# An output projection with twelve of its sixteen row tiles in Strassen's form, on one Trainium2 core

## The chip, the cores and the metric

The kernel runs on one core of a Trainium2 chip. The engines are named as in the profile: PE (TensorE, the matrix engine; PEld are its weight loads), DVE (VectorE), ACT (ScalarE), POOL (GpSimd) and SP (SyncE, which here only issues DMAs). The metric is the time of one execution on the device in microseconds, the median of several runs. Row times such as 1690.58 are microseconds from the start of the profiled span.

## The reference

The input x has 2048 rows (tokens) of 640 columns. The result mixes two blocks with a gate:

```python
g = sigmoid((x * gate_w).sum(-1, keepdims=True))
# a: attention, 32 heads of 20 columns
q, k, v = split(x @ wqkv)
p = softmax(q @ k.T * 20 ** -0.5)          # for each head
a = concat_heads(p @ v) @ wo               # the output projection, 640 x 640
# b: an MLP across the tokens
h = layernorm(x)                           # over the columns
b = (gelu(h.T @ w1 + b1) @ w2 + b2).T      # w1: 2048 x 1728, w2: 1728 x 2048
return g * a + (1 - g) * b
```

The change concerns `@ wo` alone: o, the heads' results (2048 x 640), times wo.

## The kernel before

**Precision.** Every float32 operand of a product is split into a high and a low part (`hi_lo`), and a product of two operands is three products on PE: high x high, high x low, low x high. One "product" below is one such matrix instruction.

**Stages.** First come the projections to q, k and v, then the MLP, together with part of the score maxima, then the attention loop: 16 pairs of heads (p), 32 iterations (it) each, in which ACT takes the exponentials. The attention's unnormalised results go to DRAM (`o_d`), the row sums to `l_d`, and the reciprocals of the row sums, repeated for each of a head's 20 columns, to `r_d`; for the last four heads (`LAST`) the reciprocals go to `rc_d` in a single copy, and are spread when they are read. The value projection in an early stage already has Strassen's form (`v_sums`, `v_head`, `v_body`, `v_tail`; `v_mm` at L498 writes its products): two row tiles by two halves of the contraction by two halves of the columns, seven sub-products instead of eight, with sums of x made on POOL and sums of the weights made on DVE.

**The output projection.** o is read back from DRAM transposed, as blocks of 128 columns of o (the contraction, five blocks) by rows. A *pair* q is 256 rows, two row tiles of 128. `e_load(q)` reads the first four blocks of pair q and the matching reciprocals (two loads of 512 KB, in two buffers each); `e_high` multiplies them and makes the high part, `e_low` the low part. The fifth block has its own tiles, of 512 rows each: `l_load` reads it with the reciprocals that are in `r_d`, `l_rest` reads the last four heads' reciprocals from `rc_d`, broadcast over the 20 columns of each head, `l_high` and `l_low` normalise and split. wo is loaded and split during the loop (`load_wo`, L1073) into `woh` and `wol`.

In the loop's last pair of heads `first_row` computes tile 0 and half of tile 1 (four blocks) between the attention's products, and POOL normalises pairs 0 to 2 (`e_high`, `e_low` at it 5, 20, 25). After the loop the other half of tile 1 is computed, then `pv_flush` finishes the attention, and then tiles 2 to 15 follow in order. `a_tile` (L1263) issues a tile's products: 24 for four blocks (four blocks x three passes x two halves of 320 columns), six more for the fifth block, which is accumulated with the rest from tile 8 on and done apart for tiles 0 to 7. Each tile takes its two PSUM banks in turn from four sets (`two`; `one1` and `one0`; the two `s`; `s3` and `pv`), and the `evac` that it returns multiplies by the gate and adds to the MLP's share (`tys`, loaded by `y_load`) on DVE, one instruction for each 320 columns (L1290). The row tile is stored when it is complete.

**What sets the order.** From L368 on ACT and DVE, from L455 on POOL and SP, and from the beginning PE run in the order in which the code issues (`manual_schedule`). Each of these five queues works in order; what the queues wait for follows from the tiles. The last reciprocals come late: the row sums of the last pair are stored after `pv_evac`, read back (`last_load`, L1019), inverted on DVE (`last_recip`, L1025), stored to `rc_d` from ACT's queue and read from there four times by `l_rest`.

## Time and profile before

| | |
|---|---|
| median of the runs | 1761.11 us (3 runs, 1760.94 to 1762.33) |
| the profiled execution | 1759.53 us |
| its span, first to last instruction | 1757.7 us |
| granted TensorE clock | 1.00 |
| PE busy | 1750.8 us |
| ACT busy | 1489.7 us |
| DVE busy | 1251.8 us |
| weight loads (PEld) | 1082.7 us |
| POOL busy | 682.6 us |
| DMA | 229.39 MB, mean 131 GB/s |

The page's busy time of an engine is the time in which at least one of its instructions ran. Matrix instructions overlap each other, so a row's duration is longer than the step from one to the next. A row of a timeline has start, length, engine, line of the kernel, instruction, result <- operands, shapes and count; in brackets stands the idle time of that engine just before it, and what released it. The DVE rows of L1290 are the evacuations. Queue rows (SPq, ACTq, POOL DMA) are issues of transfers, not the transfers.

### The profile page before, as it was taken

What the parts mean: (1) busy time and instruction counts of PE and PEld (TensorE: products, weight loads), DVE (VectorE), ACT (ScalarE), POOL (GpSimd) and SP (SyncE); (2) the same over time, 40 slices, a digit from 0 to 9 for tenths busy, and PEclk for the clock granted to TensorE, in tenths of its full rate; (3) what the DMA queues carried; (4) which work ended last, traced back from release to release, by engine and by line L of the source; (5) the groups of instructions that cost most, each with busy time, mean ns of one, the idle gap of its engine ahead of it and who ended that gap; (6) DMA issues with size and microseconds to landing.
All of it is one profiled execution on the core that took longest, in us unless ns stands there. A gap on an engine that the chain in (4) does not pass through costs nothing.

```text
span 1757.7 us, 39430 instructions
## 1 busy us (share of the span) xinstructions
PE 1750.8 (100%) x14972; PEld 1082.7 (62%) x14972; DVE 1251.8 (71%) x2443; ACT 1489.7 (85%) x2547; POOL 682.6 (39%) x936
## 2 busy tenths in 40 slices
PE   9999999999999999999999999999999999999999
PEld 7898899999999999533333333333333333333379
DVE  6633399988999899677767776776777777767336
ACT  5444388888888886899999999999999999999941
POOL 1434587789887777111211111121322122111410
PEclk9999999999999999999999999999999999999999
DMA  9868865476675564424313224043263144301445
GB/s 328 298 231 265 281 174 157 141 191 195 188 195 150 142 195 132 106 62 107 66 38 91 48 66 98 13 104 79 46 144 71 31 101 75 72 20 44 143 145 183
DMA packets 160945, 229.39 MB, mean 131 GB/s; under 512 B 66684, under 2 KB 97292, under 8 KB 157328
## 3 DMA queue, kind: packets, MB, share of 16 engines
q1 hardware_dynamic: 142606, 199.10, 40.6%
q0 software_dynamic: 14928, 21.86, 5.2%
q10 hardware_dynamic: 3220, 5.90, 1.1%
q8 instruction: 118, 1.93, 0.5%
q14 instruction: 73, 0.60, 0.1%
HBM read 171.07 MB, written 55.36 MB: 129 GB/s over the span
## 4 chain that ended last, share of the span: by engine, by line
PE 99%; DVE 0%; DMA 0%; ACT 0%; issue 0%; SPq 0%; ACTq 0%; DVEq 0%
PE pv L1065 29%; PE st L1164 23%; PE s L213 11%; PE y L49 10%; PE u L49 10%; PE qk L55 8%; PE v L501 4%; PE a L1284 1%; PE a_one L1284 1%; PE a_pv L1284 1%; PE a_s L1284 1%; PE a L49 0%; DMA xr<-in_xT_dram 0%; DVE mx L219 0%; PE y L894 0%
## 5 line engine op out<-in xcount | busy, mean ns | idle before, releaser
L219 DVE TENSOR_REDUCE mx<-s 128x1 f32<-128x512 f32 x1280 | 835.2, 687 | 281.8 <-PE s L213 147.0
L1182 ACT ACTIVATE p<-st 128x512 f32<-128x512 f32 x1022 | 560.5, 612 | 0.0
L1065 PE MATMUL pv<-p,v 128*32 128x512 f32 x4088 | 544.5, 605 | 0.0
L1171 ACT ACTIVATE p<-st 128x1024 f32<-128x1024 f32 x511 | 529.8, 1037 | 1.2 <-PE st L1164 1.1
L1164 PEld LDWEIGHTS st<-qs_True,ks_True 62*128 62x128 f32 x2044 | 243.8, 185 | 432.9 <-ACT p L1171 426.8
L1164 PE MATMUL st<-qs_True,ks_True 62*128 62x512 f32 x2044 | 494.0, 445 | 0.0
L213 PE MATMUL s<-ks_False,qs_False 60*128 60x512 f32 x1152 | 318.5, 391 | 0.3 <-ACT p L1182 0.2
L44 POOL TENSOR_TENSOR wl<-wr,wh 128x512 fp32r<-128x512 f32 x228 | 275.3, 1218 | 61.9 <-ACT wh L41 48.8
L238 DVE CUSTOM_DVE_ANT_0 ov<-s,ov 128x512 f32<-128x512 f32 x384 | 264.0, 688 | 36.5 <-PE s L213 25.2
L228 ACT ACTIVATE ov<-s 128x512 f32<-128x512 f32 x384 | 228.8, 598 | 62.4 <-PE s L213 54.3
L213 PE MATMUL s<-sk,sq 60*128 60x512 f32 x896 | 281.4, 394 | 0.0
L1046 POOL DMA_DIRECT2D l_d<-oev x124 | 60.4, 494 | 390.5 <-DVE oev L1038 387.8
L49 PE MATMUL y<-gh,wh 64*128 64x320 f32 x896 | 198.1, 305 | 0.0
L1065 PEld LDWEIGHTS pv<-p,v 128*32 128x32 f32 x4088 | 80.5, 108 | 187.0 <-issue 175.3
L49 PE MATMUL y<-gh,wl 64*128 64x320 f32 x832 | 191.6, 305 | 0.0
L49 PE MATMUL y<-gl,wh 64*128 64x320 f32 x832 | 191.5, 305 | 0.0
L213 PEld LDWEIGHTS s<-ks_False,qs_False 60*128 60x128 f32 x1152 | 189.0, 184 | 2.9 <-ACT p L1182 0.7
L49 PE MATMUL u<-hh,wh 64*128 64x320 f32 x864 | 186.0, 304 | 0.0
L49 PE MATMUL u<-hl,wh 64*128 64x320 f32 x864 | 185.9, 304 | 0.0
L41 ACT ACTIVATE wh<-wr 128x512 fp32r<-128x512 f32 (+3 forms) x247 | 146.8, 598 | 41.6 <-DMA wr<-in_wqk_dram 15.5
L213 PEld LDWEIGHTS s<-sk,sq 60*128 60x128 f32 x896 | 166.2, 186 | 14.9
L49 PE MATMUL u<-hh,wl 64*128 64x320 f32 x800 | 174.6, 305 | 0.0
(217 smaller groups left out, 2424.2 us busy)
## 6 DMA issues: line engine op xcount, KB each, us to landing
wr<-in_w_dram SPq DMA_DIRECT2D x192, 256.0 KB
ks_True<-k_d SPq DMA_DIRECT2D x96, 160.0 KB
qs_True<-q_d SPq DMA_DIRECT2D x192, 80.0 KB
qs_False<-q_d SPq DMA_DIRECT2D x96, 80.0 KB
v_d<-vt SPq DMA_DIRECT2D x32, 212.0 KB
sk<-k_d SPq DMA_DIRECT2D x42, 160.0 KB
sq<-q_d SPq DMA_DIRECT2D x84, 80.0 KB
v<-v_d SPq DMA_DIRECT2D x15, 424.0 KB
```

What stands on the lines that cost most here:

```text
L41: nc.scalar.activation(hi, src, AF.Copy)
L44: (lo_eng or nc.vector).tensor_sub(lo, src, hi.bitcast(F32))
L49: nc.tensor.matmul(ps[k], a[r], b[r], start=start, stop=stop)
L55: nc.tensor.matmul(ps, a, b, start=(i == 0 and k == 0), stop=(i == n - 1 and k == 2))
L213: nc.tensor.matmul(ps, qs[half][r, t * P:(t + 1) * P], ks[r, kc * 512:(kc + 1) * 512], start=True, stop=True)
L219: nc.vector.tensor_reduce(mx[:, slot, j, t: t + 1], ps, axis=AX.X, op=OP.max)
L228: nc.scalar.activation(over[j, kc], ps, AF.Relu)
L238: nc.vector.tensor_tensor_reduce(ov, ps, ov, 1.0, -3.0e38, OP.add, OP.max, mx[:, slot, j, t: t + 1])
L1065: nc.tensor.matmul(pv[r: r + 32, :], v_tiles[p][:, kt, VW * j: VW * j + 32], pt[j, c], start=(kt == 0), stop=(kt == NT - 1))
L1164: nc.tensor.matmul(ps, ks[r, kt * P:(kt + 1) * P], qs[qh][r, c * 512:(c + 1) * 512], start=True, stop=True)
L1171: nc.scalar.activation(pt, ps, AF.Exp, scale=SCALE)
L1182: nc.scalar.activation(pt, ps, AF.Exp, scale=SCALE)
```

## The change

Tiles 4 to 15, that is pairs 2 to 7, get Strassen's form over the first four blocks. For a pair, X, Y and Z are three PSUM banks of 320 columns. X takes the first product, then, accumulating, T2, T3 and T4, and is read by an evacuation after each of the four; Y takes one product, Z the product of T1 and later the one with the fourth sum of the weights. The sums of o (T1 to T4) are made by `t_sums` on POOL and split by `t_split` (high part on ACT, low part on DVE). `pair` issues a pair's first five sub-products and, in between, the last two (`foot`) of the pair before it. The sums of wo are made on POOL in the loop (`wo_load` at pair 14, it 8; `wo_sum` at pair 14, it 16, 20, 24, and pair 15, it 11).

Pair 3 is normalised on POOL in the loop, as pairs 0 to 2 are, and its load moves from it 29 to it 23; `t_sums` for pairs 2 and 3 follow there. Pairs 4 to 7 are normalised by `prep`: multiplication, sums and low part on POOL, high part on ACT, where DVE had the multiplication and the low part before. The fifth block is accumulated with the rest for tiles 8 to 15 in three of four half-tiles; the fourth (odd tile, right half) and tiles 0 to 7 (`fifth`) have products of their own, in the two banks of the tile `two`. Tile 3 is computed in two halves inside pair 2. `l_rest(3)` and `l_rest(1)` are issued after `prep(4)`, and the tiles of `l_high` come from other pools.

The core of the diff:

```diff
+    def t_sums(q):
+        raw, rb = o_keep[q]
+        r11, r12, r21, r22 = (raw[:, 2 * k: 2 * k + 2, n * P:(n + 1) * P] for k in range(2) for n in range(2))
+        t = [rb[:, j].rearrange("p (k s) -> p k s", k=2) for j in range(4)]
+        nc.gpsimd.tensor_sub(t[T1], r12, r11)
+        nc.gpsimd.tensor_sub(t[T2], r22, t[T1])
+        nc.gpsimd.tensor_sub(t[T3], r22, r12)
+        nc.gpsimd.tensor_sub(t[T4], r21, t[T2])
+    def t_split(q):
+        raw, rb = o_keep.pop(q)
+        hi, lo = t_hl[q] = t_tiles[q % 2]
+        hi_lo(hi, lo, rb, hi_eng=nc.scalar)
...
+    def wo_sum(n):
...
+        nc.gpsimd.tensor_tensor(dst, a, b, op=op)
...
+        hi_lo(hi, lo, dst, hi_eng=nc.gpsimd, lo_eng=nc.gpsimd)
...
+            if p == NP - 2 and it == 8:
+                wo_load()
+            if p == NP - 2 and it in (16, 20, 24):
+                wo_sum((it - 16) // 4)
             if p == NP - 1:
-                if it in (0, 14, 18, 29):
-                    e_load((0, 14, 18, 29).index(it))
+                if it == 11:
+                    wo_sum(3)
+                if it in (0, 14, 18, 23):
+                    e_load((0, 14, 18, 23).index(it))
...
+                if it in (5, 20, 25, 27):
+                    q = (5, 20, 25, 27).index(it)
+                    e_high(q, lp if q >= 2 else ap, nc.gpsimd)
+                    if q >= 2:
+                        o_keep[q] = o_raw[q, "e"]
                     e_low(q, nc.gpsimd)
+                    if q >= 2:
+                        t_sums(q)
...
+    def prep(q):
...
+        nc.gpsimd.tensor_mul(raw, raw, rb)
+        nc.scalar.activation(oh, raw, AF.Copy)
+        t_sums(q)
+        nc.gpsimd.tensor_sub(ol, raw, oh.bitcast(F32))
...
+    def ev(t, i, ps):
+        cols = slice(i * HALF, (i + 1) * HALF)
+        nc.vector.scalar_tensor_tensor(tys[t][:, cols], ps, g_t[:, t:t + 1], tys[t][:, cols], op0=OP.mult, op1=OP.add)
+        got(t, i)
...
+    def pair(q, fill=(), filler=()):
+        t0, t1 = 2 * q, 2 * q + 1
+        five = q >= Q0
+        X, Y, Z = o_ps[q] = [o_bank(q, k) for k in range(3)]
+        v_mm(X, [(o_x(q, 0, k), o_w(0, k)) for k in range(2)], True)
+        ev(t0, 0, X)
+        v_mm(Y, [(o_x(q, 0, 2 + k), o_w(0, 2 + k)) for k in range(2)] + [(l_x(t0), o_w(0, NC - 1)) for _ in range(five)], True)
+        ev(t0, 0, Y)
+        if q > X0:
+            foot(q - 1, 0)
+        for f in fill[:1]:
+            f()
+        v_mm(X, [(o_t(q, T2, k), o_s(2, k)) for k in range(2)], False)
+        ev(t1, 0, X)
+        if q > X0:
+            foot(q - 1, 1)
+        for f in fill[1:]:
+            f()
+        v_mm(Z, [(o_t(q, T1, k), o_s(1, k)) for k in range(2)], True)
+        ev(t1, 1, Z)
+        for f in filler[:1]:
+            f()
+        v_mm(X, [(o_t(q, T3, k), o_s(3, k)) for k in range(2)], False)
+        ev(t1, 1, X)
+        for f in filler[1:]:
+            f()
+        if five:
+            two = psum.tile([P, 2, 512], F32, tag="two", bufs=1, name=f"l{t1}")
+            v_mm(two[:, 0, :HALF], [(l_x(t1), o_w(1, NC - 1))], True)
+            ev(t1, 1, two[:, 0, :HALF])
+    def foot(q, k):
+        if k == 0:
+            v_mm(X, [(o_t(q, T4, k), o_w(1, 2 + k)) for k in range(2)] + [(l_x(t0), o_w(1, NC - 1)) for _ in range(five)], False)
+            ev(t0, 1, X)
+        else:
+            v_mm(Z, [(o_x(q, 1, 2 + k), o_s(4, k)) for k in range(2)] + [(l_x(t1), o_w(0, NC - 1)) for _ in range(five)], False)
+            ev(t1, 0, Z)
...
+    def fifth(t):
+        two = psum.tile([P, 2, 512], F32, tag="two", bufs=1, name=f"l{t}")
+        for i in range(2):
+            v_mm(two[:, i, :HALF], [(l_x(t), o_w(i, NC - 1))], True)
+        for i in range(2):
+            ev(t, i, two[:, i, :HALF])
...
     first()
     pv_flush()
+    for q in (2, 3):
+        t_split(q)
     e_load(4)
-    l_tiles()
-    e_high(3, lp)
-    e_low(3)
     last_recip()
-    for q in (2, 0):
+    l_load(2)
+    l_load(0)
+    e_load(5)
+    for q in (2, 0):
-        l_load(q)
-    e_load(5)
+        l_rest(q)
     for q in (3, 1):
         l_load(q)
-    for q in (2, 0, 3, 1):
+    a_tile(2, range(NC - 1))()
+    prep(4)
+    for q in (3, 1):
         l_rest(q)
...
+    for q in range(X0, NT // 2):
+        fill = {X0: [lambda: third(0), lambda: third(1)], Q0 - 1: [lambda: l_high(2), lambda: l_low(2)]}.get(q, [])
+        filler = [lambda t=t: fifth(t) for t in (2 * (q - Q0), 2 * (q - Q0) + 1)] if q >= Q0 else []
+        pair(q, fill, filler)
+        if X0 < q < NT // 2 - 1:
+            t_split(q + 1)
+            if q + 3 < NT // 2:
+                e_load(q + 3)
+        if q in (3, 4, 5):
+            n = (0, 3, 1)[q - 3]
+            l_high(n)
+            l_low(n)
+            prep(q + 2)
+    for k in range(2):
+        foot(NT // 2 - 1, k)
```

X0 is 2 and Q0 is 4; `third(h)` is half h of tile 3; `o_x`, `o_t`, `o_w` and `o_s` pick the operands.

More of the change, by code (lines that the diff above doesn't have):

```diff
@@ new lines, in parts, with got @@
+    def parts(t, i):
+        if t < 2 * X0:
+            return 1
+        own = 1 if t % 2 == 0 and i else 2
+        return own + (1 if t < 2 * Q0 or t % 2 and i else 0)
+    left = {(t, i): parts(t, i) for t in range(NT) for i in range(2)}
+    def ev(t, i, ps):
+        cols = slice(i * HALF, (i + 1) * HALF)
+        nc.vector.scalar_tensor_tensor(tys[t][:, cols], ps, g_t[:, t:t + 1], tys[t][:, cols], op0=OP.mult, op1=OP.add)
+        got(t, i)
+    def got(t, i):
+        left[t, i] -= 1
+        rows = slice(t * P, (t + 1) * P)
+        if t >= NT - 2:
+            if not left[t, i]:
+                put = nc.scalar if (t, i) == (NT - 2, 1) else nc.sync
+                put.dma_start(out[rows, i * HALF:(i + 1) * HALF], tys[t][:, i * HALF:(i + 1) * HALF])
+        elif not left[t, 0] and not left[t, 1]:
+            nc.sync.dma_start(out[rows, :], tys[t])
@@ new lines, in o_x, with o_t, o_w, o_s @@
+    def o_x(q, n, c):
+        return [e[:, c, n * P:(n + 1) * P] for e in o_hl[q]]
+    def o_t(q, j, k):
+        return [e[:, j, k * P:(k + 1) * P] for e in t_hl[q]]
+    def o_w(i, c):
+        return [e[c][:, i * HALF:(i + 1) * HALF] for e in (woh, wol)]
+    def o_s(j, k):
+        return [e[:, k] for e in w_sums[j]]
+    o_ps = {}
+    def o_bank(q, k):
+        tag = (("s3", "pv", "one0"), ("one1", "s", "s"))[q % 2][k]
+        return psum.tile([P, HALF], F32, tag=tag, bufs=2 if tag == "s" else 1, name=f"o{q}_{k}")
@@ new lines, in l_x @@
+    def l_x(t):
+        return [e[:, 0, (t % 4) * P:(t % 4 + 1) * P] for e in l_hl[t // 4]]
+    def pair(q, fill=(), filler=()):
[28 more added lines that the diff above has]
+            ev(t1, 1, two[:, 0, :HALF])
```

84 lines of the change are left out of this document (45 added, 39 removed).

## The prediction

> **What bounds the kernel now.** I read the page first, then the busy time by stages of the last 60 us, and then the engines' timelines of that stretch, because the change lies almost wholly in the part after the attention loop. Page and stages (each cell: busy us and, in brackets, instructions; then clock, DMA share, GB/s):
>
> ```profile
> PE 1750.8 (100%) x14972; PEld 1082.7 (62%) x14972; DVE 1251.8 (71%) x2443; ACT 1489.7 (85%) x2547; POOL 682.6 (39%) x936
> PE 99%; DVE 0%; DMA 0%; ACT 0%; issue 0%; SPq 0%; ACTq 0%; DVEq 0%
> 1700.00:1720.00 20.00, 20.00 (x138) 20.00 (x137) 11.87 (x17) 3.77 (x5) 0.00 (x0) 1.00 0.67 203
> 1720.00:1740.00 20.00, 20.00 (x139) 20.00 (x138) 15.43 (x27) 3.00 (x4) 0.00 (x0) 1.00 0.56 206
> ```
>
> TensorE is busy over the whole span and carries 99% of the chain that ended last. In the tail it is busy 20 of 20 us at clock 1.00, with the weight loads equally full, while VectorE has 5 to 8 us free in 20. So a removed product of the tail is worth its full issue step, and a wait added to TensorE costs its full length. The pace and the end of that stretch:
>
> ```profile
> 1687.62 0.41 PE L1284 MATMUL a<-woh,ohe 128*128 128x320 f32 x1
> 1690.58 0.56 PE L1284 MATMUL a_one<-woh,ohe 128*128 128x320 f32 x2
> 1753.89 0.31 PE L1284 MATMUL a<-woh,oll 128*128 128x320 f32 x1
> 1754.24 0.55 DVE L1290 SCALAR_TENSOR_TENSOR oy<-a,g_t,oy 128x320 f32<-128x320 f32 x1 [1.65 <-PE a L1284]
> 1754.82 0.37 ACTq L1293 DMA_DIRECT2D out_dram<-oy  x1
> ```
>
> From 1690.58 to 1753.89 run tiles 2 to 15: 14 x 24 products of the four blocks and 16 x 6 of the fifth, 432 in all, thus 431 steps of 0.147 us. The last product starts at 1753.89, its evacuation at 1754.24 (0.35 later), the last store at 1754.82; the span ends at 1757.7.
>
> **What is saved.** A pair of tiles had 2 x 24 products over the four blocks and has 7 x 6 in Strassen's form; the fifth block stays at 6 a tile. Six pairs save 36 products: 36 x 0.147 = 5.3 us. Whatever follows the last product (3.8 us) keeps its form: one evacuation of 320 columns and a half-row store.
>
> **What hides at no cost.** The sums of the output weights, the third and fourth pair's normalisation and their t_sums go to POOL inside the loop:
>
> ```profile
> 1629.39 1.96 POOL L1046 DMA_DIRECT2D l_d<-oev  x4 [23.64 <-DVE oev L1038]
> 1636.97 2.38 POOL L1120 TENSOR_TENSOR ole<-ore,ohe 128x1024 fp32r<-128x1024 f32 x1
> 1645.65 0.33 PE L49 MATMUL a<-woh,ohe 64*128 64x320 f32 x2
> 1659.88 1.94 POOL L1046 DMA_DIRECT2D l_d<-oev  x4 [11.91 <-DVE oev L1038]
> 1669.78 2.39 POOL L1112 TENSOR_TENSOR ore<-ore,rbe 128x1024 f32<-128x1024 f32 x1
> 1672.23 1.04 POOL L1116 CAST ohe<-ore 128x1024 fp32r<-128x1024 f32 x1
> 1673.35 2.41 POOL L1120 TENSOR_TENSOR ole<-ore,ohe 128x1024 fp32r<-128x1024 f32 x1
> 1691.73 2.04 POOL L1049 DMA_DIRECT2D o_d<-oev  x4 [15.98 <-DVE oev L1038]
> ```
>
> POOL's gaps there are 23.6, 11.9 and 16.0 us. A wo_sum is two two-input operations and a copy on 640 columns, no more than the 1024-column set 2.41 + 1.04 + 2.39 = 5.8; three fall in the second half of the last pair but one, into or just ahead of the first gap, one into the second. The extra normalisation (5.8) and eight subtractions of t_sums (0.74 each, a row below shows it: 5.9) take 11.7 of the last gap, so POOL ends about 1688, before its o_d stores at 1691.73. These and the m_d store keep their places; the r_d stores come later by up to two wo_sums (12), and what reads them, e_load(0), is wanted by POOL only after the 1629.39 row. The cover is the 6 us between POOL's first normalised block (1636.97 + 2.38) and the product that reads it (1645.65); beyond it each microsecond late would be one of TensorE's. The earlier e_load(3) waits for the buffer that POOL gives back when it goes on to the 1669.78 operation, as before, now with the last six y loads behind it on SP; their tiles (10 to 15) are used from pair 5 on. I count zero, between 0 and 1 us.
>
> **What it adds: work on VectorE in program order.** Its order is written out by hand, so it runs as the code stands. By the code the tail before has 45 evacuations (one, two for each of 14 tiles, 16 for the fifth block of tiles 0 to 7) and after it 67 (five, 42 for six pairs, 20 for the fifth block), and each pair's bank X is read three times between products that accumulate in it. So TensorE now waits for VectorE within a pair. Rows for the prices:
>
> ```profile
> 1693.69 1.23 DVE L1120 TENSOR_TENSOR ole<-ore,ohe 128x1024 fp32r<-128x1024 f32 x1 [1.12 <-ACT ohe L1114]
> 1697.34 0.55 DVE L1026 RECIPROCAL rl_last<-rl_last 128x64 f32<-128x64 f32 x1 [2.42 <-DMA rl_last<-l_d]
> 1697.81 0.91 DVE L1290 SCALAR_TENSOR_TENSOR oy<-a_one,g_t,oy 128x320 f32<-128x320 f32 x2
> 1698.64 1.00 DVE L1290 SCALAR_TENSOR_TENSOR oy<-a,g_t,oy 128x320 f32<-128x320 f32 x2
> 1701.79 1.22 DVE L1112 TENSOR_TENSOR ore<-ore,rbe 128x1024 f32<-128x1024 f32 x1 [2.15 <-DMA rbe<-r_d]
> 1702.93 0.54 DVE L1290 SCALAR_TENSOR_TENSOR oy<-a_s,g_t,oy 128x320 f32<-128x320 f32 x1
> 1710.16 0.69 DVE L1112 TENSOR_TENSOR orl<-orl,rbl 128x512 f32<-128x512 f32 x1 [0.42 <-DMA rbe<-r_d]
> 1711.55 0.69 DVE L1120 TENSOR_TENSOR oll<-orl,ohl 128x512 fp32r<-128x512 f32 x1 [0.70 <-ACT ohl L1114]
> 1712.16 1.00 DVE L1290 SCALAR_TENSOR_TENSOR oy<-a_one,g_t,oy 128x320 f32<-128x320 f32 x2
> ```
>
> (a) *Pair 2.* TensorE starts a_tile(2) at 1690.58; it, X, Y and half of tile 3 are 48 products, to 1697.6. T2 accumulates in X, after X's evacuation. On VectorE this stands behind last_recip, which waits for the round trip of the row sums until 1697.34 (same place as before: the subtraction at 1693.69 gives way to two of t_split, done by about 1696, inside the wait), and behind both evacuations of tile 2. It is the third evacuation, the one at 1698.64, done at 1699.2. TensorE waits 1.6 us. Before, the same wait was harmless: tiles 3 and 4 had banks of their own.
>
> (b) *Pair 3.* From 1699.3 come 30 products of pair 2 and 36 of pair 3, to about 1709.1. Then T3 wants T2's evacuation, and ahead of that one stands l_high(2)'s multiplication, whose operand is the broadcast load of the last reciprocals:
>
> ```profile
> 1697.93 0.35 ACTq L1027 DMA_DIRECT2D rc_d<-rl_last  x1
> 1703.68 2.71 ACTq L1148 DMA_DIRECT2D rbl<-rc_d  x4
> 1710.11 0.34 SPq L1143 DMA_DIRECT2D orl<-o_d  x1
> SPq L1143 <- DMA rbl<-rc_d: 7.7, 2, 5.4
> 1713.33 0.69 DVE L1112 TENSOR_TENSOR orl<-orl,rbl 128x512 f32<-128x512 f32 x1 [0.16 <-DMA rbl<-r_d]
> ```
>
> The broadcasts go out at 1703.68, when rc_d has landed; SP's next issue at 1710.11 is released by a broadcast, and VectorE's multiplication starts at 1710.16. So the first landed about 1710.1. The change issues it from the same landing. Multiplication 0.61 (1711.55 to 1712.16), evacuation 0.55 and 0.06 of signal: T3 at 1711.4, a wait of 2.3 us. Bounds: nothing if the load lands by 1708, 3.3 if a microsecond later.
>
> (c) *Between pairs 3/4, 4/5, 5/6* VectorE does, before it reaches the next pair's X: the last evacuation (0.20 after the product's step, then 0.47), t_split's subtraction 1.14 (1701.79 to 1702.93), l_high with ScalarE's copy 1.39 (1710.16 to 1711.55), l_low 0.61, X's evacuation 0.55 and the signal 0.06: 4.42. TensorE has 21 products (3.09) until T2 of pair 4, and 24 (3.53) until T2 of pairs 5 and 6. Waits: 1.33 + 0.89 + 0.89 = 3.1. Pair 7 has no l block ahead: 2.4 against 3.5, no wait.
>
> (d) *The pair bank "two", four times.* After fifth() of the odd tile the next three products take "two" again, a tile with one buffer, so they wait for both halves' evacuations. The first half's evacuation is running when fifth's last product ends, so the second's starts 0.26 later, takes 0.55, and with the signal that is 0.87; four times 3.5. If the first half alone had to be read, 0.40 each.
>
> (e) *Restarts and POOL.* The same Strassen form already stands in the value projection:
>
> ```profile
> 65.46 0.42 ACT L529 ACTIVATE sn<-v 128x322 f32<-128x322 f32 x1
> 65.94 0.41 PE L501 MATMUL v<-wvh,vT 128*128 128x322 f32 x1 [0.88 <-ACT sn L529]
> 66.19 0.31 PE L501 MATMUL v<-wvl,vT 128*128 128x322 f32 x1
> 82.37 0.75 POOL L446 TENSOR_TENSOR vr<-vx 128x256 f32<-128x256 f32 x1
> 83.20 1.61 POOL L447 TENSOR_TENSOR vr<-vx,vr 128x256 f32<-128x256 f32 x1
> 84.77 0.74 POOL L448 TENSOR_TENSOR vr<-vx 128x256 f32<-128x256 f32 x1
> 72.33 1.23 DVE L44 TENSOR_TENSOR vT<-vr,vT 128x1024 fp32r<-128x1024 f32 x1 [1.95 <-ACT vT L41]
> 82.83 1.39 DVE L44 TENSOR_TENSOR vT<-vr,vT 128x1024 fp32r<-128x1024 f32 x1 [4.37 <-ACT vT L41]
> ```
>
> TensorE goes on 0.06 after the releasing copy (65.88), and its first step after a wait is 0.25 instead of 0.147: nine waits, 0.9. And POOL and VectorE hold each other up when both work from SBUF: POOL's 256-column subtraction takes 1.61 beside VectorE's 1024-column one instead of 0.74, and that one 1.39 instead of 1.23, its start inside a running POOL operation. Beside evacuations from PSUM POOL keeps 0.74. In the new tail POOL works through prep(4) to prep(7), each 2.41 + 4 x 0.74 + 2.39. From e_load(4)'s landing (1701.8) it is busy till 1709.8 and goes straight on with the multiplication of pair 5, whose load lands near 1710, just when VectorE's l multiplication is due. Each meeting costs VectorE between 0 and the rest of the running operation, at most 2.4; a t_sums operation at most 0.74. I take 1.5 at pair 3 and 0.5 at each of the three boundaries, 3.0 (ends 0 and 4.5). [...]
>
> **Sum.** -5.3 + 1.6 + 2.3 + 3.1 + 3.5 + 0.9 + 3.0 = +9.1 us. The profiled execution took 1759.53 us for its span of 1757.7; the median of the runs is 1761.11, 1.6 higher. The difference is carried over to it: 1770.2 us. What goes away besides (VectorE's multiplications and subtractions of pairs 3 to 7, moved to POOL) only opens VectorE time that (c) already counts.
>
> **Rivals.**
> 1. *POOL never meets VectorE's subtractions.* For it: the landings decide, and they scatter by microseconds. Against: POOL is in prep for some 31 of 60 us. 6.1 us slower: 1767.2.
> 2. *VectorE is not late (not slower).* The place is the l block's multiplication and the copy behind it; if its load lands before 1708 and the chain of 4.42 shrinks below 3.1, (b), (c) and POOL's part vanish together. Left are 1.6 + 3.5 + 0.5 - 5.3 = +0.3: 1761.4. VectorE's free 5 to 8 us in 20 speak for it; the 1.39 round trip through ScalarE, which is no busy time, speaks against.
> 3. *Faster.* As 2, and "two" is handed over at no wait: only (a) with its restart remains, -3.6: 1757.5. Decides if the waits stay under 1.8 us in all. Against: (a) alone is 1.6.
> 4. *The load is later still, or the clock falls.* l_rest(3) and l_rest(1) stand on ScalarE's queue ahead of the copy of l_high(2); held until the second broadcast (VectorE's row at 1713.33, after a short wait), they push T3 and Y of pair 4: some 2 us more, 1772. Or the granted clock, 1.00 in every stage, falls after the longest wait, 2.3 + 1.5 in (b): at half of it, 12 steps cost 12 x 0.147 = 1.8 more, the same 1772. No row here has TensorE waiting that long, so nothing speaks for it but the length. [...]
>
> **How the numbers follow.** Forecast (1767.5 to 1773) 0.50; rival 1 0.15; rival 2 0.10; rival 3 0.05; rival 4 0.20. The range 1764 to 1774.5 takes in rival 1 with the broadcast a little early, and most of rival 4; it leaves out 2 and 3 and the far end of 4. A measurement of this kernel tells 0.2% (3.5 us) from no change: faster 0.05, within 0.10, slower 0.85. Within the likeliest case alone the range is 1767.5 to 1773.
>
> **What would show it.** TensorE's timeline should have waits released by VectorE's evacuations before pair 2's second group (near 1697.6), before pair 3's fourth (near 1709), before the second group of pairs 4 to 6, and four of about 0.9 before the three-product groups; 408 products in the tail from tile 1's half on, at 0.147; VectorE idle before orl until a broadcast lands; POOL subtractions well over 0.74 or VectorE's over 1.23 where they overlap; the loop ending near 1687.6 as before. The prediction is wrong if the broadcast lands before 1707, if VectorE takes evacuations in another order than written, if the waits of (c) shrink because a longer wait at pair 3 lets data gather, or if the loop itself grows.

## The result, and the profile after

The changed kernel takes 1775.88 us (median of 4 runs, 1772.45 to 1778.74) against 1761.03 (4 runs) of the kernel before: ratio 1.0082, 95% interval 1.0062 to 1.0102. A second measurement gave 1774.15 us (5 runs), ratio 1.0065 (1.0052 to 1.0078). The forecast was 1770.2, range 1764 to 1774.5: the direction is right, the loss was put at 9.1 us and is 11 to 15; the first measurement lies 1.4 us above the range, the second just inside it. The profiled execution took 1777.03 us for a span of 1775.2.

The page and the same two stages of the last 60 us (columns as before):

```profile
PE 1753.0 (99%) x14936; PEld 1081.0 (61%) x14936; DVE 1261.0 (71%) x2461; ACT 1493.9 (84%) x2552; POOL 743.5 (42%) x985
PE 91%; DMA 4%; DVE 2%; issue 1%; ACT 1%; POOL 0%; SPq 0%; ACTq 0%; DVEq 0%; POOLq 0%
1700.00:1720.00 20.00, 15.90 (x97) 15.41 (x96) 12.70 (x21) 2.64 (x3) 11.42 (x8) 0.91 0.72 219
1720.00:1740.00 20.00, 15.56 (x91) 14.57 (x91) 13.01 (x22) 5.16 (x6) 14.07 (x12) 0.91 0.45 147
```

PE was busy 20 of 20 us with 138 products; now it is busy 15.9 and 15.6 with 97 and 91, and the clock is 0.91. The page as a whole still says 99%: the loss is in one stage. What PE waits for there (us in all, times, longest):

```profile
PE o L501 <- DVE oy L1366: 8.0, 5, 3.2
PE l L501 <- DVE oy L1366: 5.3, 8, 1.1
```

PE's timeline, the first product of the half tile, the waits (of those that repeat, one of each) and the last product:

```profile
1690.84 0.41 PE L1332 MATMUL a<-woh,ohe 128*128 128x320 f32 x1
1702.01 0.53 PE L501 MATMUL o<-wsum,oTh 128*128 128x320 f32 x2 [0.92 <-DVE oy L1366]
1715.10 1.15 PE L501 MATMUL o<-wsum,oT 128*128 128x320 f32 x6 [3.19 <-DVE oy L1366]
1723.16 0.71 PE L501 MATMUL o<-wsum,oTh 128*128 128x320 f32 x2 [2.31 <-DVE oy L1366]
1729.56 0.41 PE L501 MATMUL l<-woh,ohl 128*128 128x320 f32 x1 [0.22 <-DVE oy L1366]
1731.81 0.42 PE L501 MATMUL l<-woh,ohl 128*128 128x320 f32 x1 [1.10 <-DVE oy L1366]
1736.84 1.12 PE L501 MATMUL o<-wsum,oT 128*128 128x320 f32 x6 [0.81 <-DVE oy L1366]
1749.41 0.53 PE L501 MATMUL o<-wsum,oTh 128*128 128x320 f32 x2 [0.80 <-DVE oy L1366]
1771.48 0.31 PE L501 MATMUL o<-woh,oll 128*128 128x320 f32 x1
```

All thirteen waits are for evacuations. Below, a wait is the step from one product's start to the next less 0.147, a little more than the bracket shows. In order: 1.07 us (T2 of pair 2), 3.35 (T3 of pair 3), 2.46 (T2 of pair 4), then 0.96 (T2 of pairs 5 and 6), and in each of pairs 4 to 7 0.38 (ahead of the odd `fifth`) and 1.26 (ahead of the three products behind it): 15.4 us. I call *tail* the stretch from the first product of the half tile to the end of the span. It was 70.08 us (1757.7 - 1687.62) and is 84.36 (1775.2 - 1690.84), 14.3 more. The sum closes: -5.3 saved, +15.4 waits, +1.1 for the restarts (1.4 against 0.3 before), +3.25 for two stretches in which PE's step was 0.267 instead of 0.147, and -0.1 behind the last product, is 14.3.

The clock by 5 us, with those two stretches in the second to the fourth row:

```profile
1710.00:1715.00 5.00, 1.92 (x14) 1.66 (x12) 1.11 (x3) 0.33 (x1) 1.89 (x1) 1.00 0.34 121
1715.00:1720.00 5.00, 4.90 (x23) 4.90 (x24) 4.90 (x7) 1.25 (x2) 3.79 (x2) 0.66 0.69 221
1720.00:1725.00 5.00, 2.69 (x13) 2.46 (x13) 3.35 (x6) 2.63 (x3) 4.92 (x5) 0.83 0.57 180
1725.00:1730.00 5.00, 4.78 (x27) 4.52 (x27) 3.10 (x6) 0.00 (x0) 4.84 (x5) 0.82 0.01 3
```

The rest of the 17.5 us between the two spans, 3.2 us, lies ahead of the tail. It is there already at the first product of the MLP, in code that the change does not touch. One of the MLP's groups (durations, then start of its first and last product), in the kernel before

```profile
L49 PE MATMUL u<-hh,wh x864: 299/306/310, 219.5 to 592.7; 64*128 64x320 f32 x173
```

and in the changed one:

```profile
L49 PE MATMUL u<-hh,wh x864: 299/306/310, 222.4 to 595.9; 64*128 64x320 f32 x173
```

### The profile page after: what moved, and what is told of

The parts are those of the page before. It is cut to its first block, busy times and chain, and to the rows that moved or that the text cites. A ratio compares the mean times of both kernels' runs of the same rounds, so it can differ in the third digit from the quotient of the medians.

```text
span 1775.2 us, 39486 instructions
## 1 busy us (share of the span) xinstructions
PE 1753.0 (99%) x14936; PEld 1081.0 (61%) x14936; DVE 1261.0 (71%) x2461; ACT 1493.9 (84%) x2552; POOL 743.5 (42%) x985
## 4 chain that ended last, share of the span: by engine, by line
PE 91%; DMA 4%; DVE 2%; issue 1%; ACT 1%; POOL 0%; SPq 0%; ACTq 0%; DVEq 0%; POOLq 0%
PE pv L1065 29%; PE st L1205 22%; PE s L213 11%; PE y L49 10%; PE u L49 8%; PE qk L55 5%; PE v L501 3%; PE o L501 1%; DMA wr<-in_w_dram 1%; PE l L501 1%; DMA kd_d<-evl 1%; DMA kd_d<-dh 0%; DMA rbl<-rc_d 0%; DMA xn<-in_x_dram 0%; DVE oy L1366 0%
## 5 line engine op out<-in xcount | busy, mean ns | idle before, releaser
L41 ACT ACTIVATE wh<-wr 128x512 fp32r<-128x512 f32 (+3 forms) x247 | 146.8, 598 | 41.2 <-PE y L49 15.6
```

The source lines that it names most:

```text
L41: nc.scalar.activation(hi, src, AF.Copy)
```

## The experiments

The expectations below count pairs and quarters from one (their fifth pair is pair 4, their third quarter the fifth block's tile 2); what they call the seventh row tile is tile 3.

My theory: PE waits at a few fixed places for evacuations that VectorE reaches late in its written order, and after long waits the clock falls. Rivals: GpSimd and VectorE holding each other up is the main cost; the loop grew; VectorE has too much to do in any order.

| kernel | ratio to before (95%) | tail | waits | slow steps cost |
|---|---|---|---|---|
| before, twice | | 70.08, 70.02 | 0 | 0 |
| changed | 1.0082 (1.0062-1.0102) | 84.36 | 15.4 | 3.3 |
| after_again | 1.0065 (1.0052-1.0078) | 81.95 | 14.5 | 1.6 |
| third_first | 1.0072 (1.0060-1.0085) | 81.60 | 14.5 | 1.4 |
| l1_in_y | 1.0048 (1.0036-1.0061) | 78.26 | 10.5 | 2.4 |
| keep_warm | 1.0082 (1.0069-1.0096) | 83.39 | 10.7 | 0 |
| b_early | 1.0093 (1.0080-1.0107) | 84.86 | 15.9 | 2.6 |
| pool_off5 | 1.0060 (1.0046-1.0074) | 82.65 | 15.3 | 1.5 |
| pool_none | 1.0045 (1.0033-1.0057) | 79.93 | 12.4 | 1.5 |
| stt_form | 1.0076 (1.0063-1.0088) | 83.96 | 15.8 | 2.3 |
| all_four | 1.0059 (1.0046-1.0072) | 80.62 | 12.3 | 1.8 |
| spread | 1.0013 (1.0004-1.0022) | 72.96 | 4.4 | 2.9 |
| spread_stt | 1.0022 (1.0012-1.0032) | 72.41 | 4.9 | 1.6 |
| slots | 1.0016 (1.0003-1.0029) | 72.60 | 5.8 | 1.5 |
| spread_pool_none | 0.9985 (0.9976-0.9993) | 67.74 | 2.4 | 0 |
| spread_pieces | 1.0002 (0.9993-1.0011) | 69.56 | 3.5 | 0 |
| slots_pieces | 1.0014 (1.0005-1.0024) | 72.14 | 6.2 | 0 |
| spread_late | 0.9997 (0.9988-1.0006) | 69.21 | 2.6 | 0 |

Tail, waits and slow steps (us) are each kernel's profiled execution; they leave out what varies ahead of the tail. pool_off5, pool_none and spread_pool_none leave out a part of the work and serve as probes alone.

**before_again, after_again.** No edit.

> The kernel before once more, for a second profile. Theory that the 3.2 us by which the changed kernel's first half-tile product came later are chance of the early part: the profiles of the kernels with the change so far have it at 1690.84, 1690.13, 1689.82, 1689.69 and 1689.74, and the kernel before would have it between 1688 and 1690.5, later than the 1687.62 of its first profile, as that run was 1.3 us below the median of its runs. Rival, that the parts added to the loop cost 2 to 3 us: it is at 1687 to 1688 again. The stretch from there to the span's end is 70.0 to 70.2 us by both.

> The changed kernel once more. Theory of late evacuations, with GpSimd's multiplication for the sixth pair delaying one or the other VectorE instruction, as in the three variants: the waits of pairs 4 to 7 for the pair bank (0.38 and 1.26 us each) and the 0.96 us in front of T2 of pairs 5 and 6 come out the same to 0.02 us; the waits in front of T2 of pair 2, T3 of pair 3 and T2 of pair 4 share 6 to 7 us among them in one way or the other; the tail is 81 to 84.5 us. Rival, that these three waits are fixed: 1.07, 3.35 and 2.46 us again.

The kernel before had its first half-tile product at 1689.28 this time and a tail of 70.02, so its early part varies by 1.7 us or more between two executions. In the 17 profiles with the change it lies between 1688.70 and 1692.36. (In third_first it is at 1688.70, in l1_in_y at 1688.84, in keep_warm at 1688.71; the 1690.13, 1689.82 and 1689.69 of the expectation are later products of the same half tile.) From the MLP's first product to it are 1468.1 and 1468.3 us before, and 1467.9 to 1470.0 with the change: what the loop adds costs 0.2 us in the mean. The kernel before has 2 profiles and its mean is 1.8 us lower; its timed runs of 1760.8 to 1762.9 (less 1.8 around the span and 70.05 of tail) put it at 1689 to 1691, so I count no loss there. The changed kernel again, PE's three first waits, then VectorE's multiplication that T3 of pair 3 waits behind, and the GpSimd operation beside it:

```profile
1701.66 0.53 PE L501 MATMUL o<-wsum,oTh 128*128 128x320 f32 x2 [1.25 <-DVE oy L1366]
1715.23 0.99 PE L501 MATMUL o<-wsum,oT 128*128 128x320 f32 x4 [3.66 <-DVE oy L1366]
1721.62 0.53 PE L501 MATMUL o<-wsum,oTh 128*128 128x320 f32 x2 [0.64 <-DVE oy L1366]
1712.49 2.22 DVE L1190 TENSOR_TENSOR orl<-orl,rbl 128x512 f32<-128x512 f32 x1 [2.97 <-DMA rbl<-rc_d]
1711.82 2.35 POOL L1351 TENSOR_TENSOR ore<-ore,rbe 128x1024 f32<-128x1024 f32 x1
```

The bank's 0.38 and 1.26 us and the 0.96 come out the same to 0.02. The three others are 1.41, 3.82 and 0.79: 6.0 in sum, as expected, shared in another way. In the first profile GpSimd met the subtraction between pairs 3 and 4:

```profile
1713.89 0.69 DVE L1190 TENSOR_TENSOR orl<-orl,rbl 128x512 f32<-128x512 f32 x1 [4.02 <-DMA rbl<-rc_d]
1717.14 2.46 DVE L44 TENSOR_TENSOR oTl<-rbe,oTh 128x1024 fp32r<-128x1024 f32 x1
1716.13 2.39 POOL L1351 TENSOR_TENSOR ore<-ore,rbe 128x1024 f32<-128x1024 f32 x1 [4.24 <-DVE oll L1120]
1718.59 1.59 POOL L1138 TENSOR_TENSOR rbe<-ore 128x256 f32<-128x256 f32 x1
```

**third_first.**

```diff
-        fill = {X0: [lambda: third(0), lambda: third(1)], ...
+        fill = {X0: [lambda: [third(0), third(1)]], ...
```

> Both halves of the seventh row tile are computed before T2 of pair 2, not one before and one behind it. Theory of late evacuations: the wait in front of T2 of pair 2 (1.07 us in the changed kernel's profile) is covered by the 15 products of the second half (2.2 us); nothing else changes, since the half behind T2 covered nothing that waits: the tail (from the first half-tile product to the span's end, 84.4 us) is shorter by 1.0 to 1.1 us. Rival, that the wait in front of T3 of pair 3 is fixed by a transfer's landing and not by where PE is: PE then comes to that wait 1.1 us sooner and waits 1.1 us more (4.4 us instead of 3.35), and the tail is the same within 0.3 us.

```profile
1713.46 1.97 PE L501 MATMUL o<-wsum,oT 128*128 128x320 f32 x6 [4.80 <-DVE oy L1366]
```

The wait of pair 2 is gone, and T3 of pair 3 waits 4.96: it starts 24.76 us into the tail, between the 24.26 and 25.08 of the changed kernel's two profiles. The rival is right: that wait is for a transfer, and what PE gains ahead of it, it loses there. The tail is that of after_again within 0.4 us; the first profile of the changed kernel has a longer wait at T2 of pair 4 (2.46 instead of 1.05) and one slow stretch more.

**l1_in_y.**

```diff
-            two = psum.tile([P, 2, 512], F32, tag="two", bufs=1, name=f"l{t1}")
-            v_mm(two[:, 0, :HALF], [(l_x(t1), o_w(1, NC - 1))], True)
-            ev(t1, 1, two[:, 0, :HALF])
+            v_mm(Y, [(l_x(t1), o_w(1, NC - 1))], True)
+            ev(t1, 1, Y)
```

> The three products of the odd tile's fifth block go into the pair's own bank Y, long read by then, and not into the pair bank that waits for both evacuations. Theory of late evacuations: of the term (d), 1.26 us and two restarts fall away in each of pairs 4 to 7, and the 0.38 us before each second fifth stays: the tail is shorter by 4 x 1.3 = 5.2 us, less what the DVE chain between pairs takes back (T2 of pairs 5 and 6 waited 0.96 us; PE now comes 1.3 us sooner by its side, DVE's evacuation of these products 1.3 us sooner too): 4.0 to 5.4 us. Rival, that PE's loss is set by DVE's total work in these pairs: the waits move to T2 of the next pair, and the tail is shorter by under 2 us.

PE's waits, as shown above for the changed kernel (us in all, times, longest):

```profile
PE o L501 <- DVE oy L1366: 8.3, 4, 4.4
PE l L501 <- DVE oy L1366: 0.9, 4, 0.2
```

The four waits of 1.26 are gone, those of 0.39 stay, and T2 of pairs 5 and 6 waits 1.44 instead of 0.96: 4.1 us of waits less. The tail is 3.7 and 6.1 us shorter than in the two profiles of the changed kernel, and the ratio falls by 0.002 to 0.003. The theory holds: the handing over of the bank pair `two` is the largest single item.

**keep_warm.** `warm(q, n)` writes 3n products into `two`.

```diff
+        if q == Q0:
+            warm(q, 5)
         v_mm(X, [(o_t(q, T2, k), o_s(2, k)) for k in range(2)], False)
...
+        if q == Q0 - 1:
+            warm(q, 7)
         v_mm(X, [(o_t(q, T3, k), o_s(3, k)) for k in range(2)], False)
```

> 21 extra products are put in front of T3 of pair 3 and 15 in front of T2 of pair 4, in the waits of 3.35 and 2.46 us; their results are used nowhere. Theory that the two stretches of steps of 0.267 us come from the idle time before them: the steps stay at 0.147 us and the tail is shorter by about 3 us (2.4 to 3.2), since 21 x 0.147 = 3.1 us and 15 x 0.147 = 2.2 us fit into the waits; from 0.1 to 0.5 us may go for evacuations that come later. Rival, that the clock falls for another cause (what the core did before, or the load of the other engines): the slow steps stay, the extra products themselves run slower, and the tail is the same or up to 1 us longer.

```profile
1715.00:1720.00 5.00, 5.00 (x36) 4.98 (x35) 4.20 (x7) 1.73 (x3) 1.62 (x3) 1.00 0.73 237
1720.00:1725.00 5.00, 4.87 (x32) 4.40 (x30) 3.72 (x9) 0.80 (x1) 4.86 (x3) 1.00 0.15 49
```

Every step is 0.147, the clock 1.00, in all five runs 1.000 over the span against 0.998 and 0.999 in the nine runs of the changed kernel: the slow steps come from the idle time, which is thus shown. The expected gain of some 3 us did not come. The extra products take 36 x 0.147 = 5.3 us themselves, and the waits fall by 4.7 and 3.8 us only (10.7 against 15.4 and 14.5): from the first to the last product are 78.3 us against 80.6 and 78.3. Besides, the span ends 5.1 us after the last product instead of 3.7; the difference lies behind the issue of the last store, and no row says why.

**b_early.** The loads of quarters 3 and 1 go behind pair 2, and:

```diff
     l_load(2)
-    l_load(0)
-    e_load(5)
-    for q in (2, 0):
-        l_rest(q)
+    l_rest(2)
+    put[0] = nc.scalar
+    e_load(5)
+    l_load(0)
+    l_rest(0)
+    put[0] = nc.sync
```

> The broadcast of the fifth block's third quarter is issued right behind the store that it reads, the loads of the sixth pair and of the first quarter are issued behind it from ACT's queue, and those of the other two quarters behind pair 2. Theory that T3 of pair 3 waits because this broadcast lands behind the 2.4 MB of other loads that are in flight: it lands 2 to 4 us sooner, the wait of 3.35 us falls under 1.3 us, and with it the first of the two stretches of slow steps goes (1.5 us): the tail is shorter by 2 to 5 us. Rival, that the broadcast is slow by itself (5.5 us from the issue of the last to its landing): it still lands behind 1712, the wait stays over 2.3 us, and the tail is shorter by under 1 us. Risk on both: the transfers of the sixth pair now come later, and POOL's work for it with them, which costs nothing unless T2 of pair 5 waits for it.

```profile
1711.55 1.15 PE L501 MATMUL o<-wsum,oT 128*128 128x320 f32 x6 [0.24 <-DVE oy L1367]
1715.27 0.42 PE L501 MATMUL o<-woh,ole 128*128 128x320 f32 x1 [1.87 <-POOL ole L1355]
1722.65 0.53 PE L501 MATMUL o<-wsum,oTh 128*128 128x320 f32 x2 [3.14 <-DVE oy L1367]
```

The broadcast came 2 us sooner and the wait of 3.35 fell to 0.40, as the theory said, but the tail did not: X of pair 4 then waited 2.03 for GpSimd's low part (its copy stood on ACT behind the loads that I had put there) and T2 of pair 4 3.45. A wait taken away at one place is paid at the next.

**pool_off5, pool_none.** pool_off5 skips `tensor_mul` and `t_sums` in `prep(5)`; pool_none has in every `prep`:

```diff
-        nc.gpsimd.tensor_mul(raw, raw, rb)
         nc.scalar.activation(oh, raw, AF.Copy)
-        t_sums(q)
-        nc.gpsimd.tensor_sub(ol, raw, oh.bitcast(F32))
+        nc.scalar.activation(ol, raw, AF.Copy)
```

> GpSimd's multiplication and its four subtractions for the sixth pair (pair 5) are left out, so that pair's rows are not normalised and its sums not formed; all other work stays. Theory that VectorE's operations between SBUF tiles wait while GpSimd's operation runs: the two multiplications and the subtractions of VectorE between 1711 and 1722 take 0.68 to 0.70 us and 1.22 us each, none takes 1.1 to 2.5 us, the wait in front of T3 of pair 3 is at most 3.4 us and that of pair 4's T2 at most 1.1 us, and the tail is shorter than the changed kernel's by 1.5 to 3 us (the longer waits bring the slow steps too, some 1.5 us of it). Rival, that the longer durations of VectorE come from the transfers in flight: they stay, and so does the tail within 0.5 us.

> All of GpSimd's work for pairs 4 to 7 is left out: their rows are not normalised, their sums are not formed, and their low parts are copies that ACT makes. Everything else of the changed kernel stays. Theory that GpSimd's operations hold VectorE's up and that this is a part, not the whole: VectorE's operations between SBUF tiles all take 0.68 to 0.70 and 1.22 to 1.23 us, the waits in front of T2 of pair 2, T3 of pair 3 and T2 of pair 4 sum to 4 to 5.5 us (6.0 and 6.9 us in the two profiles of the changed kernel), the pair bank's waits of 1.26 and 0.38 us and the 0.96 us of pairs 5 and 6 stay, and the tail is 79.5 to 82 us against 81.95 and 84.36. Rival, that the hold is the main cost: the tail is under 78 us. Rival, that it costs nothing: the tail is over 82 us.

The multiplication ahead of T3 of pair 3 in pool_off5, with GpSimd's operation beside it,

```profile
1713.45 1.93 DVE L1190 TENSOR_TENSOR orl<-orl,rbl 128x512 f32<-128x512 f32 x1 [3.54 <-DMA rbl<-rc_d]
1712.50 2.34 POOL L1356 TENSOR_TENSOR ole<-ore,ohe 128x1024 fp32r<-128x1024 f32 x1
```

and in pool_none:

```profile
1712.34 0.69 DVE L1190 TENSOR_TENSOR orl<-orl,rbl 128x512 f32<-128x512 f32 x1 [3.09 <-DMA rbl<-rc_d]
1713.55 1.31 PE L501 MATMUL o<-wsum,oT 128*128 128x320 f32 x6 [2.26 <-DVE oy L1364]
```

The first failed as a test: the hold moved to the fifth pair's subtraction. With none of GpSimd's work for pairs 4 to 7 VectorE's multiplication takes 0.69, the first three waits are 1.41, 2.43 and 0 (3.8 in sum, a little under the 4 to 5.5 expected), and the tail is 79.93, 2 to 4.4 us shorter: a part, not the whole.

**stt_form.** In `l_high`, `l_low` and `t_split`, as here:

```diff
-        nc.vector.tensor_mul(raw, raw, rb)
+        nc.vector.scalar_tensor_tensor(raw, raw, 1.0, rb, op0=OP.mult, op1=OP.mult)
```

> VectorE's multiplications and subtractions between SBUF tiles in the tail (the fifth blocks' product and low part, the low part of the sums) are written in the instruction form of the evacuations (a, times 1.0, times or minus b), which kept its 0.55 us beside GpSimd's work in every profile; nothing else is changed, same operands, same places. Theory that the hold is one of the two-tensor form against GpSimd's operation (the VectorE operation ended 0.54 to 0.55 us after GpSimd's ended in four profiles): these operations now take their plain time (about 0.7 us for 512 columns, about 1.2 to 1.3 us for 1024) while GpSimd runs, the wait in front of T3 of pair 3 loses 0.8 to 1.7 us, and the tail is shorter by 1 to 3 us than in the profiles of the changed kernel (81.95 and 84.36 us). Rival, that the hold comes from both engines reading and writing SBUF, whatever the form: durations of 1.1 to 2.5 us stay, and so does the tail.

```profile
1713.54 2.38 DVE L1198 SCALAR_TENSOR_TENSOR oll<-orl,ohl 128x512 fp32r<-128x512 f32 x1
1712.97 2.40 POOL L1354 TENSOR_TENSOR ore<-ore,rbe 128x1024 f32<-128x1024 f32 x1 [0.98 <-DMA rbe<-r_d]
```

The rival is right: the form does not matter. The subtraction is held as long (2.38), and ends 0.55 after GpSimd's operation. What the evacuations have different is that one operand is in PSUM; their smaller size, 320 columns, was not tried apart from it. spread_stt repeats it on the kernel below:

> The same with VectorE's operations in the form of the evacuations. If that form is not held up by GpSimd: the waits are 0.5 to 2 us less than in the kernel with the work spread alone, tail 66.5 to 69 us. Rival (the form makes no difference): the same tail within 0.5 us.

The tail is the same (72.41 and 72.96); operations of 2 us and more stay.

**all_four, spread.** Both halves of tile 3 first, Y for the three products, `l_high(n)` behind Y's evacuation and `l_low(n)` behind T4's inside the pair that needs it, `t_split(q + 1)` behind T3 of pair q, the even `fifth` ahead of T1. all_four also moved the loads and left `prep(q + 2)` at the end of a pair; spread keeps the loads and has `prep(q + 1)` behind `l_low(n)`. In spread:

```diff
+    def split(q):
+        if X0 < q < NT // 2 - 1:
+            t_split(q + 1)
...
+    def l_end(q):
+        if q < 7:
+            l_low((0, 3, 1)[q - Q0])
+            prep(q + 1)
...
         ev(t0, 0, Y)
+        if Q0 <= q < 7:
+            l_high((0, 3, 1)[q - Q0])
         if q > X0:
             foot(q - 1, 0)
...
```

`l_end(q)` is called ahead of T2 of pairs 4 to 7, `split(q)` behind T3.

> All of it together: both halves of the seventh row tile ahead of T2 of pair 2; the odd tile's three products into bank Y; the broadcast of the third quarter first, the sixth pair's loads behind the fifth's POOL work; and the blocks' normalisation and the split of the next pair's sums spread over each pair, not in a row between two pairs, with the even fifth one step earlier in pairs 5 to 7. Theory of late evacuations: of the 15.4 us of waits in the changed kernel's tail 1 to 4 us are left (most of it at T3 of pair 3 and in pair 4), no step of 0.267 us remains, and the tail is 70.1 - 5.3 + (1 to 4) + about 1 for restarts = 67 to 70 us; the kernel takes 1758 to 1761.5 us, at or under the kernel before. Rival, that VectorE's total work in pairs 4 to 6 (12 evacuations of 0.55 us, 1.2 us and 1.4 us, 9.2 us of a pair's 9.7 us) with GpSimd's delays is the bound: waits of 1 us or more stay in each of pairs 4 to 6, and the tail is 71 us or more.

> As the kernel with all of it together, but the loads in the changed kernel's order, and each pair's normalisation (the multiplication, ACT's copy, GpSimd's work) in the order in which the parts are needed: the fifth block's copy on ACT stands ahead of the sixth pair's, which made PE wait 8.15 us. Theory of late evacuations: no wait over 1.5 us is left, waits in all are 1.5 to 4 us, no step of 0.267 us remains, the tail is 67 to 70 us, and the kernel takes 0.1 to 0.3% less than the kernel before. Rival, that VectorE and GpSimd together have too much to do in pairs 4 to 6: waits of over 1 us in each of these pairs, a tail of over 71 us, and the kernel is slower than before.

PE's longest wait in all_four,

```profile
1728.60 0.64 PE L501 MATMUL l<-woh,ohl 128*128 128x320 f32 x1 [8.00 <-ACT ohl L1192]
```

and in spread, with the VectorE and GpSimd operations ahead of it:

```profile
1716.05 0.43 PE L501 MATMUL o<-woh,ohl 128*128 128x320 f32 x1 [2.61 <-ACT ohl L1191]
1712.89 2.39 DVE L1190 TENSOR_TENSOR orl<-orl,rbl 128x512 f32<-128x512 f32 x1 [2.78 <-DMA rbl<-rc_d]
1712.37 2.37 POOL L1351 TENSOR_TENSOR ore<-ore,rbe 128x1024 f32<-128x1024 f32 x1 [0.72 <-DMA rbe<-r_d]
```

all_four has 8.15 of its 12.3 us of waits from one mistake of order: the fifth block's copy stood on ACT behind that of pair 5, whose data came late. spread puts it ahead, with the changed kernel's loads; its tail is 9.0 and 11.4 us shorter than those of the changed kernel, and four waits are left, two of 0.4 us and two in pair 4. The expectation of a gain fails: pair 4 waits 2.77 us for the block whose multiplication took 2.39 us beside GpSimd's operation instead of 0.69, and slow steps follow.

**slots.** Also `t_split(4)` inside pair 3, the fifth block's multiplication behind pair 4's X, its products behind T3, `fifth` tiles moved to pairs 5 to 7.

> As the kernel with the work spread, and in addition: the split of the fifth pair's sums goes into pair 3, where VectorE stood idle for 2.8 us before the fifth block's multiplication; that multiplication comes behind the evacuation of T3 of pair 3 and of X of pair 4, so that neither waits for the broadcast; pair 4's three products with that block are appended to Y behind its T3, and the eight fifth tiles move to pairs 5 (two), 6 (three) and 7 (three). Theory of late evacuations: the waits of 2.77 and 0.83 us and the 2.9 us of slow steps behind them go, as nothing on PE needs the broadcast before 1717; waits in all are 0.5 to 2.5 us, no step of 0.267 us remains, the tail is 70.05 - 5.3 + (0.5 to 2.5) + about 0.8 = 66 to 68.1 us and the kernel takes 2 to 4 us less than the kernel before. Rival, that VectorE, held up by GpSimd, is too late in pair 4 in any order: waits of 2 us or more before T2 or T4 in pairs 4 and 5, slow steps behind them, and a tail of 69 us or more.

```profile
1723.54 0.41 PE L501 MATMUL o<-woh,ole 128*128 128x320 f32 x1 [2.17 <-POOL ole L1354]
1739.59 0.41 PE L501 MATMUL l<-woh,ohl 128*128 128x320 f32 x1 [2.17 <-DVE oy L1366]
```

The rival is right: the waits at pair 4 went, and one for GpSimd's low part and one behind two held VectorE operations took their place. This order gains nothing over spread's (tail 72.60 against 72.96).

**spread_pool_none, spread_pieces, slots_pieces.** spread with the edit of pool_none; then spread and slots, each with all of GpSimd's work, but the low part and

```diff
-        nc.gpsimd.tensor_mul(raw, raw, rb)
+        for c in range(NC - 1):
+            nc.gpsimd.tensor_mul(raw[:, c], raw[:, c], rb[:, c])
```

> The same left out of the kernel with the work spread over the pairs (tail 72.96 us in its profile, 4.4 us of waits and about 2.9 us of slow steps). Theory that what is left there is VectorE being held up by GpSimd: VectorE's multiplication ahead of pair 4 takes 0.69 instead of 2.39 us and the subtraction 0.69 instead of 1.20, so the waits of 2.77 and 0.83 us fall to about 1.1 us together, the slow steps of 2.9 us go or halve, and the tail is 67.5 to 69.5 us, under the 70.05 us of the kernel before. Rival, that the broadcast's landing or VectorE's own load sets it: waits of 3 us or more stay in pair 4, and the tail is over 71 us.

> GpSimd's multiplications and low-part subtractions for pairs 4 to 7 are each made in four operations of 256 columns (0.74 us) instead of one of 1024 (2.39 us); all work is done. Theory that VectorE waits for the end of the one GpSimd operation that is under way: no VectorE operation between SBUF tiles takes more than 0.74 us over its plain 0.69 or 1.22 us, the multiplication ahead of pair 4 takes at most 1.45 instead of 2.39 us, and the tail is between the 67.74 us without GpSimd's work and the 72.96 us with it, at 69 to 71 us: the kernel is within 0.1% of the kernel before. Rival, that the total of GpSimd's work sets it: VectorE's operations are held as long as before in sum, GpSimd takes 0.6 us longer for each of its operations, and the tail is 73 us or more.

> The same in the kernel with the fifth pair's split in pair 3 (tail 72.60 us, of its waits 2.33 us for GpSimd's low part of the sixth pair, 2.44 us for an evacuation behind two held operations). Theory of the hold by one operation: the two held operations in pair 6 (2.12 and 1.74 us) and the one in pair 3 (2.31) fall to at most 1.45 and 1.95 us, the wait of 2.44 us goes under 1.2; the wait for GpSimd's low part falls only as GpSimd itself is held less, and may grow as four operations take 0.6 us longer; tail 69 to 72 us. Rival, the total of the work: 72.5 us or more.

VectorE's and GpSimd's rows of spread_pieces, the count of GpSimd's standing behind the x:

```profile
1711.84 0.69 DVE L1190 TENSOR_TENSOR orl<-orl,rbl 128x512 f32<-128x512 f32 x1 [2.62 <-DMA rbe<-r_d]
1713.27 1.08 DVE L1120 TENSOR_TENSOR oll<-orl,ohl 128x512 fp32r<-128x512 f32 x1 [0.28 <-ACT ohl L1191]
1711.89 4.72 POOL L1352 TENSOR_TENSOR ore<-ore,rbe 128x256 f32<-128x256 f32 x4 [0.58 <-DMA rbe<-r_d]
```

Without GpSimd's work for pairs 4 to 7, which a usable kernel needs, the tail is 67.74, within the expected 67.5 to 69.5, and the time is 0.15% under that of the kernel before: GpSimd's work costs spread 5.2 us of tail, and none of spread's waits is for GpSimd's own results, so this is the hold and the slow steps behind it. In four pieces 3.4 of the 5.2 us come back, with all work done: 69.56, as expected, ratio 1.0002. GpSimd now waits too (four pieces took 4.72 instead of 2.9). slots_pieces did not follow (72.14): four of its five waits, 4.2 of 6.2 us, are for GpSimd's low part, which pieces make no sooner.

**spread_late.** spread_pieces, with the order of the parts in a table (filler1 stands behind T3, hook ahead of T4, fill0 ahead of T2, fill1 ahead of T1), here of pairs 3 and 4; pair 4's products with the fifth block join Y ahead of T1:

```diff
+        3: {"fill1": [sp[3]], "filler1": [hi[2]]},
+        4: {"hook": [lo[2], hi[0]], "fill0": [lo[0], pr[5]], "filler0": [fi[0]], "filler1": [sp[4], fi[1]]},
```

> As the spread kernel with GpSimd's operations in pieces, and: the split of the fifth pair's sums moves into pair 3 where VectorE is idle (2.62 us ahead of the broadcast's landing); the fifth block's multiplication comes behind T3's evacuation of pair 3, its low part behind X's of pair 4; and pair 4's three products with that block are appended to Y ahead of T1. Theory that the order is at fault: the waits of 1.32, 0.72 and 0.77 us in pair 4 go, waits in all are 0.5 to 1.5 us, and the tail is 66.5 to 68.3 us, 2 to 3.5 us under the kernel before. Rival, that VectorE's load in pairs 3 and 4 is: other waits of 2 us or more in sum take their place in pairs 4 and 5, and the tail is 69 us or more.

The three waits went; 0.64, 0.78 and 1.17 took their place, at GpSimd's low part, at the next block's and at the bank `two`. Tail 69.21, ratio 0.9997: nothing that can be told from no change. By the tails it is 0.8 us better than before; no kernel with all the work done is faster beyond the noise.

## Why the prediction was right or wrong

The sign, the places and the mechanism are right: each of the terms (a) to (d) is a wait at the product named, released by an evacuation. Point by point, the first profile's number, then the second's:

- *What is saved, 5.3, and the loop, 0 to 1*: right (36 products fewer on the page; 0.2 us in the mean).
- *(a) 1.6*: 1.07 and 1.41. The reciprocal came sooner, and as third_first shows the term is no loss of its own: it is given back at T3 of pair 3.
- *(b) 2.3 and (c) 3.1, with the 3.0 for GpSimd*: 8.4 foreseen, 7.7 and 6.5 measured (3.35 + 4.38; 3.82 + 2.73). pool_none has them without the hold: 2.43 and 1.94. So (b) was sized rightly, (c) by 1.2 too large (T2 of pair 4 does not wait there; by the sum the slow steps ahead of it, 1.5 us, fill the time, which was not tried apart), and the hold was put at the right size: the sums differ by 3.4 and 2.2 us. That is luck in part, since it fell on pairs 3 and 4 alone, mostly on T2 of pair 4 in the first profile, and not on three boundaries. In nine profiles with this work of GpSimd's (the changed kernel's two, pool_off5, stt_form, all_four, spread, spread_stt, slots and spread_pieces) a held operation of 512 columns ended 0.54 to 0.56 us after GpSimd's, one of 1024 columns 1.07 to 1.09, and cutting GpSimd's operation cut the hold: the longest operation of 512 columns took 2.39 us in spread and 1.27 in spread_pieces.
- *(d) 3.5 is the step that failed*: 6.6. I had the first half's evacuation run beside fifth's second half. It starts only behind both:

```profile
1730.74 1.01 DVE L1366 SCALAR_TENSOR_TENSOR oy<-l,g_t,oy 128x320 f32<-128x320 f32 x2 [0.78 <-PE l L501]
```

  One row for both evacuations, 0.78 us idle before it, released by the last product of both. So the bank comes free 1.26 us after fifth's last step, not 0.87. And the wait of 0.38 ahead of the odd `fifth` was not in the sum at all: I had looked at one user of `two` and not at the one before it. Together +3.1 us of the miss.
- *(e) 0.9*: 1.1, thirteen waits instead of nine.
- *The clock, rival 4, is the second step that failed*. It was one half of a rival that got 0.20, at a price of 1.8 us, with the remark that nothing spoke for it but the length. No row ahead of the prediction showed the half clock or the twelve steps of that price: I had supposed them. The clock fell after the wait of 3.35, and once more after 2.46 in the first profile: 3.25 us, and 1.6 in the second, after 3.82. The runs show the half (in the first profile a granted clock of 0.50 from 1717 to 1719, steps of 0.267 for 0.147, 13 and 14 of them), and after shorter waits too, below. The forecast's own sum had a wait of 3.8 us there, (b) and GpSimd's 1.5, and by these runs should have had the fall in it.

With the measured sizes the sum is 9.1 + 3.1 for (d) + 3.25 (1.6) for the clock + 0.2 for (e) - 1.2 (2.0) for (a) to (c) and the hold - 0.1 = 14.3 (11.9), the two tails. Rival 2 (VectorE not late) and rival 3 (faster) are approached only when the order is changed and the hold taken out: spread_pool_none, with 2.4 us of waits left.

## What to carry to other kernels

This form, with 36 products fewer, put 67 evacuations where 45 had stood; list for each PSUM bank who must have read it before it is written again, and where that read stands in the reading engine's order, before counting what is saved. Put work that waits for a late transfer behind the evacuations that the matrix engine needs next, not ahead of them, and cut long operations of GpSimd in pieces where VectorE works between SBUF tiles beside it and nothing waits for GpSimd's own result (3.4 us gained in spread, 0.5 in slots). Price a wait of over 2 us on a busy matrix engine above its length: of the nine kernels above with a single such wait eight have 1.4 to 2.9 us of slow steps, and slots_pieces, with 2.07 us, has none.
